# Moving weight subtractions off GpSimd and giving weight conversion fixed places in an attention and gated-MLP kernel

## The chip, the cores and the metric

The kernel runs on one core of a Trainium2 chip. The metric is the time of one execution in microseconds (us) on the device; the kernel before has a median of 754.77 us over three runs. A core has engines that work side by side, each through its own queue in order: TensorE (PE) multiplies matrices, VectorE (DVE) and GpSimd (POOL) do elementwise work, ScalarE (ACT) does activations and copies, SyncE (SP) and GpSimd issue the DMA transfers used here. Data lies in on-chip memory (SBUF) with 128 partitions; PE writes its sums to a second on-chip memory (PSUM).

## The reference

```python
# q, k, v: (4, 8, 576, 64)
scores = matmul(q, k.T) / sqrt(64)
rel = pos[:, None] - pos[None, :]
x = (log1p(abs(rel)) / log1p(max(pos, 1))[:, None])[..., None]
bias = relu(x @ w1 + b1) @ w2            # 32 hidden units, 8 heads
scores = scores + bias.transpose(2, 0, 1)[None]
attn = exp(scores - max(scores)); attn = attn / (sum(attn) + 1e-9)
x = (attn @ v).transpose(0, 2, 1, 3).reshape(2304, 512)
h = x @ w_in                             # (2304, 2048)
g = h * tanh(softplus(h))
out = g @ w_out                          # (2304, 512), float32
```

The weights w_in and w_out are double precision at the input, all else is float32.

## The kernel before

Every product is made of three: PE multiplies a rounded "high" part, which is fast, and a "low" part is the value minus its high part. So q, k, the weights, x and g are each split into hi and lo by a copy that rounds and a subtraction.

The program has three stages, each written out step by step, and each engine takes its work in the order of the code.

The bias stage, 0 to 62 us of the profiled run, makes a bias table per head from 36 groups of rows: DVE and ACT make ht (L488, L490), PE multiplies (bps, L517), ACT evacuates (L497, L498), and the table goes to DRAM and back. Between the groups lie the loads of the first two pairs of heads, the first three score steps (SOFT_AT), and the splits of q and k for pair 0 on DVE.

The attention stage, 62 to 326 us, goes over 16 pairs (two heads of one batch), five steps x = 0 to 4 each (n = 5i + x), which are the row blocks 0, 1, 4, 2, 3. A step does scores (L220, PE) into one of two PSUM buffers s, adds the bias and takes the row maxima on DVE (add_bias, L236, which frees s), exponentiates on ACT (L251), transposes the block of two steps earlier (PE L282 and L285, ACT copies L283, L289) and multiplies by v (L315, L319). The first product of step x = 2 is twelve matmuls long and serves as the mark of a pair below. At x = 4, load_hi and load_raw fetch q and k of the pair after the next. At x = 1 and x = 2, split_k and split_q on POOL subtract for the next pair: in the first pair both come at n = 3.

Beside this the weights are converted. A weight tile of 128x512 arrives as 64-bit words (load_weights, SP). Four operations make a float32: high (a multiplication, DVE L120 or ACT L118), low (a shift, DVE L123), a merge (DVE L125) and the sign (DVE L127). Then split_weights copies the high part (ACT L137) and subtracts for the low part on POOL (L138, tiles wli and wlo). 16 tiles are converted in the attention stage, one operation per step in a rotation of four steps that runs past the five of a pair; the other 16 are converted in the MLP. w64 and w32 have two buffers each.

The MLP, 326 to 752 us, goes over units of 12 matmuls for h (hidden, L594) and 12 for y (project, L632), where y lags three units behind h. Between the two, a gate: ACT exp (L599), DVE L600 and L601, ACT L609 and L610, DVE L611 and L612, ACT ghi (L613), and the subtraction for glo (L614), which runs on POOL for the first 23 units and on DVE after. Block 1 of x is split in the first eight units (split_x). The first segment's y accumulators are copied out (L639) after unit 7. convert() does a whole tile at the end of a unit: in three of four units from unit 8 on, in every second one before.

Of the kernel before, what the change touches and what calls it, by code (L numbers as in the profile page):

```python
# [19 lines left out]
P = 128  # L20
# [26 lines left out]
def kernel(ctx: ExitStack, tc, qk, v, wb, w2, w_in, w_out, psia, psi4, rinv, eye, out):  # L47
# [41 lines left out]
    todo, w64, w32 = list(order), [], []  # L89
# [17 lines left out]
    def conv_weights(on_act):  # L107

        job, w = w64.pop(0)
        c = convp.tile([P, 512], F32, name="w32")
        cu = c.bitcast(U32)
        high = convp.tile([P, 512], F32, name="high", bufs=1)
        low = convp.tile([P, 512], U32, name="low", bufs=1)
        hu = high.bitcast(U32)
        if on_act:
# [4 lines left out]
        def parts():  # L122
            dve.tensor_scalar(low, w[:, :, 0], 29, None, op0=ALU.logical_shift_right)  # L123
            yield False
            dve.scalar_tensor_tensor(cu, hu, 3, low, op0=ALU.logical_shift_left, op1=ALU.bitwise_or)  # L125
            yield False
            dve.scalar_tensor_tensor(cu, hu, 0x80000000, cu, op0=ALU.bitwise_and, op1=ALU.bitwise_or)  # L127
            w32.append((job, c))
            yield True
        return parts()  # L130
# [44 lines left out]
    def split_k(i):  # L175
        kl = qk_hi[i][64:128, QW:]
        (pool if i else dve).tensor_tensor(kl, qk_raw[i][64:128], kl.bitcast(F32), op=ALU.subtract)  # L177

    def split_q(i):

        lo = q_los[i % 2]
        (pool if i else dve).tensor_tensor(lo[0:64], qk_raw.pop(i)[0:64], qk_hi[i][0:64, :QW].bitcast(F32), op=ALU.subtract)  # L182
# [147 lines left out]
    conv = []  # L330
# [26 lines left out]

    def ahead(n):
# [18 lines left out]
    def split(n):  # L377
# [131 lines left out]
    for idx in range(NB + 2):  # L509
# [94 lines left out]
    def gate(blk, fs, eng=dve):  # L604
# [9 lines left out]
        eng.tensor_tensor(glo, e, ghi.bitcast(F32), op=ALU.subtract)  # L614
# [83 lines left out]
    done = []  # L698

    def convert():  # L700

        if done:
            split_weights(done.pop())
        if w64:
            for _ in conv_weights(True):
                pass
            load_weights()
            done.append(pool)

    gate(*units[0], pool)  # L710
    hidden(*units[1])
    convert()
    gate(*units[1], pool)
    hidden(*units[2])

    for k in range(2, len(units) + LAG2):
        if k < len(units):
            blk, fs = units[k]
            f = fs[0]
            if k < FH:  # L720
                split_x(1, XPARTS[:2] if k == 2 else XPARTS[2:4] if k == 3 else XPARTS[k:k + 1])
# [14 lines left out]
            if k > 2:  # L736
# [3 lines left out]
        if 2 <= k - 1 < len(units):  # L740
            gate(*units[k - 1], pool if k < 3 * FH else dve)
        if k > 2 and (k % 4 < 3 if k >= FH else k % 2):
# [58 lines left out]
```

## Time and profile before

| | us |
|---|---|
| median of three runs | 754.77 |
| runs | 753.52, 754.77, 756.04 |
| profiled execution, its own time | 754.99 |
| its span | 752.1 |
| busy: PE / DVE / ACT / POOL | 712.2 / 514.3 / 467.9 / 181.8 |

The span is the stretch from the first to the last instruction that the profiler recorded, and 2.9 us of the execution lie around it. Busy times say how much an engine did, not whether anybody waited for it; that is read from the chain that ended last, from the waits behind single rows, and from the timeline. The granted clock of TensorE is 1.00 at 2.4 GHz and 0.50 at 1.2 GHz; its mean in this execution is 0.986.

### The profile page before, as it was taken

What the parts mean: (1) busy time and instruction counts of PE and PEld (TensorE: products, weight loads), DVE (VectorE), ACT (ScalarE), POOL (GpSimd) and SP (SyncE); (2) the same over time, 40 slices, a digit from 0 to 9 for tenths busy, and PEclk for the clock granted to TensorE, in tenths of its full rate; (3) what the DMA queues carried; (4) which work ended last, traced back from release to release, by engine and by line L of the source; (5) the groups of instructions that cost most, each with busy time, mean ns of one, the idle gap of its engine ahead of it and who ended that gap; (6) DMA issues with size and microseconds to landing.
All of it is one profiled execution on the core that took longest, in us unless ns stands there. A gap on an engine that the chain in (4) does not pass through costs nothing.

```text
span 752.1 us, 11589 instructions
## 1 busy us (share of the span) xinstructions
PE 712.2 (95%) x4144; PEld 544.4 (72%) x4144; DVE 514.3 (68%) x987; ACT 467.9 (62%) x995; POOL 181.8 (24%) x113
## 2 busy tenths in 40 slices
PE   6769999999999999899989999999999999999997
PEld 2226777777777777658767776688998888888886
DVE  7995767768677764346877777777576666665554
ACT  6877877887888787665455455555454554444443
POOL 1110443565444453402343433300100000000000
PEclk9979999999999999999998999999999999999999
DMA  8987759648866977141113311132304000010001
GB/s 276 308 256 249 242 165 298 214 161 276 258 205 186 299 242 222 45 128 37 57 56 112 112 57 56 29 113 79 90 1 120 22 0 1 1 56 1 1 0 57
DMA packets 46681, 95.68 MB, mean 127 GB/s; under 512 B 13456, under 2 KB 22304, under 8 KB 44576
## 3 DMA queue, kind: packets, MB, share of 16 engines
q1 hardware_dynamic: 43744, 74.80, 32.9%
q0 software_dynamic: 2304, 19.92, 7.8%
q8 instruction: 32, 0.52, 0.3%
q10 hardware_dynamic: 576, 0.22, 0.1%
q14 instruction: 25, 0.20, 0.1%
HBM read 73.48 MB, written 21.45 MB: 126 GB/s over the span
## 4 chain that ended last, share of the span: by engine, by line
PE 66%; DVE 17%; ACT 8%; issue 4%; DMA 2%; POOL 2%; SPq 1%; DVEq 0%; ACTq 0%; POOLq 0%
PE y L632 18%; PE h L594 17%; PE s L220 11%; PE o L315 8%; PE tp L282 6%; DVE w L127 3%; PE bps L517 3%; DVE w L125 2%; DVE e L601 2%; DVE e L612 2%; DVE e L600 2%; PE o L319 2%; DVE e L611 2%; DMA xr<-r_d 2%; ACT high L118 1%
## 5 line engine op out<-in xcount | busy, mean ns | idle before, releaser
L251 ACT ACTIVATE pt<-pt,m 128x576 f32<-128x576 f32 x144 | 112.7, 784 | 53.0 <-DVE m L236 52.4
L236 DVE CUSTOM_DVE_ANT_0 pt<-s,bias 128x576 f32<-128x576 f32 x144 | 103.7, 752 | 55.3 <-PE s L220 53.5
L613 ACT CAST ghi<-e 128x512 fp32r<-128x512 f32 x72 | 44.7, 621 | 143.7 <-DVE e L612 139.7
L632 PE MATMUL y<-who,glo 128*128 128x512 f32 x288 | 114.4, 397 | 5.9 <-POOL glo L614 5.9
L632 PE MATMUL y<-who,ghi 128*128 128x512 f32 x288 | 114.1, 396 | 4.4 <-ACT xraw L639 2.2
L632 PE MATMUL y<-wlo,ghi 128*128 128x512 f32 x288 | 113.2, 393 | 0.0
L594 PE MATMUL h<-xhi,whi 128*128 128x512 f32 (+1 forms) x320 | 80.3, 372 | 1.0 <-ACT xhi L569 0.9
L594 PE MATMUL h<-xlo,whi 128*128 128x512 f32 (+1 forms) x320 | 79.0, 368 | 0.0
L594 PE MATMUL h<-xhi,wli 128*128 128x512 f32 (+1 forms) x320 | 78.8, 368 | 0.0
L220 PE MATMUL s<-qkhi 128*128 128x288 f32 x320 | 77.1, 322 | 0.7 <-issue 0.4
L315 PE MATMUL o<-main,vt 128*64 128x320 f32 (+1 forms) x512 | 75.8, 418 | 1.2 <-DVE x L322 1.2
L600 DVE TENSOR_SCALAR e<-e 128x512 f32<-128x512 f32 x72 | 36.5, 507 | 57.5 <-ACT e L599 57.5
L220 PEld LDWEIGHTS s<-qkhi 128*128 128x128 f32 x320 | 49.5, 189 | 34.1 <-issue 28.6
L220 PE MATMUL s<-qkhi,qlo 128*128 128x288 f32 x320 | 69.1, 297 | 3.6 <-POOL qlo L182 3.6
L177 POOL TENSOR_TENSOR qkhi<-rawqk,qkhi 64x1216 fp32r<-64x1216 f32 x15 | 42.7, 2844 | 118.5 <-DMA rawqk<-in_qk_dram 55.2
L632 PEld LDWEIGHTS y<-who,glo 128*128 128x128 f32 x288 | 54.6, 190 | 22.1 <-POOL glo L614 10.9
L599 ACT ACTIVATE e<-h 128x512 f32<-128x512 f32 x72 | 42.6, 591 | 43.5 <-PE h L594 43.5
L283 ACT COPY main<-tp 128x512 f32<-128x512 f32 x128 | 68.0, 581 | 0.7 <-PE tp L282 0.2
L632 PEld LDWEIGHTS y<-who,ghi 128*128 128x128 f32 x288 | 54.5, 189 | 19.0 <-ACT ghi L613 4.2
L282 PE MATMUL tp<-ident,pt 128*128 128x128 f32 x512 | 67.4, 275 | 0.7 <-ACT main L283 0.7
L594 PEld LDWEIGHTS h<-xhi,whi 128*128 128x128 f32 x320 | 57.8, 190 | 13.5 <-ACT xhi L569 2.4
L594 PEld LDWEIGHTS h<-xlo,whi 128*128 128x128 f32 x320 | 56.9, 189 | 10.4 <-DVE xlo L571 0.4
(75 smaller groups left out, 1210.6 us busy)
## 6 DMA issues: line engine op xcount, KB each, us to landing
qkhi<-in_qk_dram POOLq DMA_DIRECT2D x16, 1216.0 KB, 8.7
bias_d<-bt SPq DMA_DIRECT2D x36, 295.5 KB
rawqk<-in_qk_dram SPq DMA_DIRECT2D x32, 304.0 KB
w<-in_w_in_dram SPq DMA_DIRECT2D x16, 512.0 KB
w<-in_w_out_dram SPq DMA_DIRECT2D x16, 512.0 KB
vt<-in_v_dram SPq DMA_DIRECT2D x16, 320.0 KB
bias<-bias_d SPq DMA_DIRECT2D x16, 288.0 KB
out_dram<-w SPq DMA_DIRECT2D x17, 256.0 KB
```

The source lines that it names most:

```text
L177: (pool if i else dve).tensor_tensor(kl, qk_raw[i][64:128], kl.bitcast(F32), op=ALU.subtract)
L220: pe.matmul(s[:, j, :SH], stat[:, q0:q0 + P], hi[:, QW + kc + j * SH:QW + kc + (j + 1) * SH], start=(k == 0), stop=(k == len(todo) - 1))
L236: dve.tensor_tensor_reduce(out=halves(pt[:, sl]), in0=s[:, :, :SH], in1=halves(bt[:, sl]), scale=-0.125, scalar=BIG, op0=ALU.add, op1=ALU. ...
L251: act.activation(ps, ps, AF.Exp, bias=m[:, u:u + 1], scale=-1.0, accum_out=sums[i][:, k:k + 1])
L282: pe.transpose(tp[:, k * P:(k + 1) * P], pt[:, c0:c0 + P], ident)
L283: act.copy(main[:, h, :, off:off + P], tp.rearrange("p (k q) -> p k q", k=4))
L315: pe.matmul(o[h * 64:h * 64 + 64, :w], vt[:, h, k, :], main[:, h, k, :], start=(k == 0), stop=False, **kw)
L594: pe.matmul(h[:, u * n:(u + 1) * n], w["i", g4, d][:, r * P:(r + 1) * P], x[:, d, :n], start=(k == 0), stop=(k == 11))
L599: act.activation(e, h, AF.Exp)
L600: dve.tensor_scalar(e, e, E20, None, op0=ALU.min)
L613: act.copy(ghi, e)
L632: pe.matmul(ys[blk][t], g[:, c0:c0 + P], w, start=((blk, f) in first and k == 0), stop=((blk, f) in last and k == 2))
```

## The change

- The subtraction for wli and wlo (split_weights) moves from POOL to DVE, 32 instructions. That for glo of the first 23 MLP units does too. So do split_k and split_q of pair 1, and its split_q moves from n = 3 to n = 4. POOL keeps the splits of q and k of the pairs 2 to 15, the multiplications of x by the reciprocals, and two additions at the end.
- In the attention stage the operations of a tile have fixed steps: high and low at x = 4, followed by the load of the next tile; the merge at x = 0; the sign at x = 1; the copy of the high part and the subtraction at x = 2. The last tile goes through the steps n = 77 to 79.
- In the MLP, ACT's high stands at the start of a unit, low, merge and sign stand on DVE between L612 and the subtraction for glo, and the split of the tile comes at the start of the next unit. A tile is taken in units 0, 2, 4, 6, 7 and then in two of three units. The loop now starts with unit 0, and split_x of block 1 is spread over units 0 to 6.
- In the bias stage load_raw(1) moves from group 14 to 26, load_hi(1) from 18 to 28, the first load of weights from 26 to 30.

```diff
-    def conv_weights(on_act):
+    def scale_high(eng):
...
+    def shift_low():
+        job, w, high = half.pop(0)
+        low = convp.tile([P, 512], U32, name="low", bufs=1)
+        dve.tensor_scalar(low, w[:, :, 0], 29, None, op0=ALU.logical_shift_right)
+        half.append((job, high, low))
+        load_weights()
...
-    def split_weights(eng):
+    def split_weights():
         act.copy(w_hi[job], c)
-        eng.tensor_tensor(w_lo[job], c, w_hi[job].bitcast(F32), op=ALU.subtract)
+        dve.tensor_tensor(w_lo[job], c, w_hi[job].bitcast(F32), op=ALU.subtract)
...
     def split_k(i):
         kl = qk_hi[i][64:128, QW:]
-        (pool if i else dve).tensor_tensor(kl, qk_raw[i][64:128], kl.bitcast(F32), op=ALU.subtract)
+        (pool if i > 1 else dve).tensor_tensor(kl, qk_raw[i][64:128], kl.bitcast(F32), op=ALU.subtract)
...
-        if (x == 2 or n == 3) and i + 1 < NPAIR:
+        if (x == 2 or n == 4) and i + 1 < NPAIR:
             split_q(i + 1)
-        for _ in range((1, 1, 1, 1, 1)[x]):
-            if not conv and w64[0][0] in order[:HALF]:
-                conv.append(conv_weights(x == 2))
-            elif conv and next(conv[0]):
-                conv.clear()
-                load_weights()
-                split_weights(pool)
+        for do in CONV.get(n, {4: (scale_high, shift_low), 0: (merge,), 1: (sign,), 2: (split_weights,)}.get(x, ())):
+            do(*((dve,) if do is scale_high else ()))
...
-        if idx == 14:
+        if idx == 26:
             load_raw(1)
-        if idx == 18:
+        if idx == 28:
             load_hi(1)
-        if idx == 26:
+        if idx == 30:
             load_weights()
...
         act.copy(ghi, e)
-        eng.tensor_tensor(glo, e, ghi.bitcast(F32), op=ALU.subtract)
+        if half:
+            convert()
+        dve.tensor_tensor(glo, e, ghi.bitcast(F32), op=ALU.subtract)
...
-    for k in range(2, len(units) + LAG2):
+    for k in range(len(units) + LAG2):
+        on = k % 3 < 2 if k >= FH else k in (0, 2, 4, 6, 7)
+        if w32:
+            split_weights()
+        if on and w64:
+            scale_high(act)
...
-        if k > 2 and (k % 4 < 3 if k >= FH else k % 2):
+        if 0 <= k - 1 < len(units):
+            gate(*units[k - 1])
+        elif half:
             convert()
```

First place, DVE around step x = 2 of pair 11, before. L236 is add_bias, in two rows an instruction, L322 the copy of an attention output, L125 the merge; pt4 belongs to step 2, the last two s to step 3.

```order
L322 COPY x_3249<-o_3155 128x256
L236 ISA pt4_3262,m_3261<-s_3252,bias4_2410 128x576
L236 ISA m_3261 128x1
L125 SCALAR_TENSOR_TENSOR w32_3198<-high_3199,low_3200 128x512
L236 ISA pt_3305,m_3304<-s_3294,bias2_2453 128x576
L236 ISA m_3304 128x1
L236 ISA pt_3305,m_3304<-s_3299,bias2_2453 128x576
```

The same place after; lines have moved by eight or ten, so that add_bias is L244, the sign L136, and the subtraction for wlo L146.

```order
L136 SCALAR_TENSOR_TENSOR w32_3165<-high_3116,w32_3165 128x512
L330 COPY x_3214<-o_3122 128x256
L244 ISA pt4_3227,m_3226<-s_3217,bias4_2388 128x576
L244 ISA m_3226 128x1
L146 TENSOR_TENSOR wlo02_3252<-w32_3165,who02_3251 128x512
L244 ISA pt_3273,m_3272<-s_3262,bias2_2434 128x576
L244 ISA m_3272 128x1
L244 ISA pt_3273,m_3272<-s_3267,bias2_2434 128x576
```

Where before a step of the rotation stood, in this pair a merge, there now stands the subtraction, which needs ACT's copy who of the same step, between the add_bias of step 2 and the two of step 3.

Second place, DVE in a unit of the MLP that converts a tile, before. L600 to L612 belong to the gate, L123 to L127 to the conversion; the subtractions stand on POOL.

```order
L600 TENSOR_SCALAR e_4669<-e_4669 128x512
L601 SCALAR_TENSOR_TENSOR e_4669<-e_4669 128x512
L611 TENSOR_TENSOR e_4620<-h_4607,e_4620 128x512
L612 TENSOR_TENSOR e_4620<-e_4620,r_4685 128x512
L123 TENSOR_SCALAR low_4698<-w64_4565 128x512
L125 SCALAR_TENSOR_TENSOR w32_4696<-high_4697,low_4698 128x512
L127 SCALAR_TENSOR_TENSOR w32_4696<-high_4697,w32_4696 128x512
```

The same after. L603, L604, L619, L620 are the gate, L122, L129, L136 the conversion, L624 is glo and L146 a weight's low part.

```order
L603 TENSOR_SCALAR e_4722<-e_4722 128x512
L604 SCALAR_TENSOR_TENSOR e_4722<-e_4722 128x512
L619 TENSOR_TENSOR e_4682<-h_4669,e_4682 128x512
L620 TENSOR_TENSOR e_4682<-e_4682,r_4738 128x512
L122 TENSOR_SCALAR low_4746<-w64_4612 128x512
L129 SCALAR_TENSOR_TENSOR w32_4750<-high_4707,low_4746 128x512
L136 SCALAR_TENSOR_TENSOR w32_4750<-high_4707,w32_4750 128x512
L624 TENSOR_TENSOR glo_4740<-e_4682,ghi_4739 128x512
L146 TENSOR_TENSOR wli30_4335<-w32_4750,whi30_4334 128x512
```

DVE has two instructions more in such a unit, and the order of the seven others is kept.

Third place, SP in pair 13, where x of the first MLP block (xraw) and the reciprocals that it is multiplied by (xr) are loaded, before.

```order
L326 DMA x_d0_80<-x_3764 128x256
L327 DMA x_d0_80<-x_3764 128x64
L163 DMA rawqk_3799<-in_qk_dram 64x1216
L164 DMA rawqk_3799<-in_qk_dram 64x1216
L166 DMA vt_3802<-in_v_dram 128x640
L340 DMA xraw_3804<-x_d0_80 128x4x512
L354 DMA xr_3843<-r_d0_84 64x2x512 x2
```

The same after.

```order
L334 DMA x_d0_80<-x_3725 128x256
L335 DMA x_d0_80<-x_3725 128x64
L171 DMA rawqk_3760<-in_qk_dram 64x1216
L172 DMA rawqk_3760<-in_qk_dram 64x1216
L174 DMA vt_3763<-in_v_dram 128x640
L347 DMA xraw_3765<-x_d0_80 128x4x512
L104 DMA w64_3771<-in_w_out_dram 128x1024
L361 DMA xr_3810<-r_d0_84 64x2x512 x2
```

A load of a weight tile, 512 KB, now stands between xraw and xr.

## Rows read from the trace of the kernel before

**Rows 1.** The page, chain that ended last: shares of the span by engine.

```profile
PE 66%; DVE 17%; ACT 8%; issue 4%; DMA 2%; POOL 2%; SPq 1%; DVEq 0%; ACTq 0%; POOLq 0%
```

**Rows 2.** Windows: stretch, its length, busy us (instructions) per engine, clock, DMA share, GB/s.

```profile
62.00:326.00 264.00, 258.60 (x1903) 195.39 (x1902) 176.22 (x416) 209.52 (x533) 113.73 (x62) 0.99 0.69 212
326.00:521.00 195.00, 182.79 (x784) 141.59 (x782) 141.77 (x209) 101.55 (x180) 56.45 (x39) 0.98 0.23 72
```

**Rows 3.** Timeline (start, length, engine, line, operation, count, wait), PE in the MLP.

```profile
346.02 0.39 PE L632 MATMUL y<-who,ghi 128*128 128x512 f32 x1
348.74 1.07 PE L594 MATMUL h<-xhi,whi 128*128 128x512 f32 x4
...
390.57 1.07 PE L594 MATMUL h<-xhi,whi 128*128 128x512 f32 x4
...
520.52 0.64 PE L594 MATMUL h<-xhi,whi 128*128 128x256 f32 x4
```

**Rows 4.** Timeline, DVE, one group of the MLP.

```profile
421.79 1.67 DVE L127 SCALAR_TENSOR_TENSOR w<-high,w 128x512 uint32<-128x512 uint32 x1
...
425.22 0.69 DVE L612 TENSOR_TENSOR e<-e,r 128x512 f32<-128x512 f32 x1
425.83 0.42 DVE L123 TENSOR_SCALAR low<-w 128x512 uint32<-128x512 uint32 x1
...
428.62 1.67 DVE L127 SCALAR_TENSOR_TENSOR w<-high,w 128x512 uint32<-128x512 uint32 x1
```

**Rows 5.** Windows, the stretch after the first y accumulators are copied out.

```profile
396.00:402.80 6.80, 6.17 (x15) 4.38 (x14) 5.10 (x9) 3.19 (x7) 1.75 (x2) 0.50 0.55 208
```

**Rows 6.** Lines by shape, DVE, 35.3 to 41.2: busy us, mean ns.

```profile
L490 DVE TENSOR_SCALAR ht<-at,bb 128x304 f32<-128x304 f32 x3 | 5.9, 2010 | 0.0
```

**Rows 7.** The same, 41.2 to 50.7.

```profile
L490 DVE TENSOR_SCALAR ht<-at,bb 128x304 f32<-128x304 f32 x2 | 0.6, 359 | 0.0
```

**Rows 8.** Lines by shape, DVE, whole span.

```profile
L177 DVE TENSOR_TENSOR qkhi<-rawqk,qkhi 64x1216 fp32r<-64x1216 f32 x1 | 1.4, 1423 | 0.0
```

**Rows 9.** Timeline, POOL and DVE, conversion in the attention stage.

```profile
99.71 2.79 POOL L182 TENSOR_TENSOR qlo<-rawqk,qkhi 64x1216 fp32r<-64x1216 f32 x1
100.08 2.97 DVE L125 SCALAR_TENSOR_TENSOR w<-high,low 128x512 uint32<-128x512 uint32 x1
...
129.93 0.68 DVE L127 SCALAR_TENSOR_TENSOR w<-high,w 128x512 uint32<-128x512 uint32 x1
```

**Rows 10.** Timeline, ACT, DVE and PE, pair 13 from its step 2.

```profile
279.23 1.84 PE L315 MATMUL o<-main,vt 128*64 128x320 f32 x12
281.41 0.28 ACT L289 COPY tail<-tp 128x128 f32<-128x128 f32 x1
281.82 0.76 DVE L236 CUSTOM_DVE_ANT_0 pt<-s,bias 128x576 f32<-128x576 f32 x1 [2.16 <-PE s L220]
284.46 0.53 PE L220 MATMUL s<-qkhi 128*128 128x288 f32 x2
...
295.81 1.84 PE L315 MATMUL o<-main,vt 128*64 128x320 f32 x12
```

**Rows 11.** Timeline, ACT, the copy of a weight's high part.

```profile
131.91 0.64 ACT L137 CAST who<-w 128x512 fp32r<-128x512 f32 x1
```

**Rows 12.** Timeline, POOL: load of q and k issued, split of k.

```profile
169.71 0.57 POOL L172 DMA_DIRECT2D qkhi<-in_qk_dram  x1 [0.46 <-PE s L220]
178.84 3.16 POOL L177 TENSOR_TENSOR qkhi<-rawqk,qkhi 64x1216 fp32r<-64x1216 f32 x1 [3.38 <-DMA rawqk<-in_qk_dram]
...
219.77 0.57 POOL L172 DMA_DIRECT2D qkhi<-in_qk_dram  x1 [0.70 <-PE s L220]
229.66 2.80 POOL L177 TENSOR_TENSOR qkhi<-rawqk,qkhi 64x1216 fp32r<-64x1216 f32 x1 [1.93 <-DMA rawqk<-in_qk_dram]
...
286.09 0.57 POOL L172 DMA_DIRECT2D qkhi<-in_qk_dram  x1 [0.67 <-PE s L220]
```

**Rows 13.** Timeline, PE, pair 15's first use of qlo.

```profile
307.43 0.85 PE L220 MATMUL s<-qkhi,qlo 128*128 128x288 f32 x2 [2.92 <-POOL qlo L182]
```

More of the change, by code (lines that the diff above doesn't have):

```diff
@@ L88 @@
     w_hi, w_lo = {}, {}
-    todo, w64, w32 = list(order), [], []
+    todo, w64, half, w32 = list(order), [], [], []
     def alloc_weights(jobs, p):
@@ L105, in load_weights @@
             w64.append((job, w))
-    def conv_weights(on_act):
+    def scale_high(eng):
         job, w = w64.pop(0)
-        c = convp.tile([P, 512], F32, name="w32")
-        cu = c.bitcast(U32)
         high = convp.tile([P, 512], F32, name="high", bufs=1)
-        low = convp.tile([P, 512], U32, name="low", bufs=1)
-        hu = high.bitcast(U32)
-        if on_act:
+        if eng is act:
             act.mul(high, w.bitcast(F32)[:, :, 1], 2.0 ** -112)
@@ L120, in conv_weights, with merge, sign @@
             dve.tensor_scalar(high, w.bitcast(F32)[:, :, 1], 2.0 ** -112, None, op0=ALU.mult)
[L122 to L130, printed above, removed]
-    def split_weights(eng):
+        half.append((job, w, high))
+    def shift_low():
[4 more added lines that the diff above has]
+        load_weights()
+    def merge():
+        job, high, low = half.pop(0)
+        c = convp.tile([P, 512], F32, name="w32")
+        dve.scalar_tensor_tensor(c.bitcast(U32), high.bitcast(U32), 3, low,
+                                 op0=ALU.logical_shift_left, op1=ALU.bitwise_or)
+        half.append((job, high, c))
+    def sign():
+        job, high, c = half.pop(0)
+        cu = c.bitcast(U32)
+        dve.scalar_tensor_tensor(cu, high.bitcast(U32), 0x80000000, cu,
+                                 op0=ALU.bitwise_and, op1=ALU.bitwise_or)
+        w32.append((job, c))
+    def split_weights():
         job, c = w32.pop(0)
@@ L176, in split_k @@
         kl = qk_hi[i][64:128, QW:]
-        (pool if i else dve).tensor_tensor(kl, qk_raw[i][64:128], kl.bitcast(F32), op=ALU.subtract)
+        (pool if i > 1 else dve).tensor_tensor(kl, qk_raw[i][64:128], kl.bitcast(F32), op=ALU.subtract)
     def split_q(i):
         lo = q_los[i % 2]
-        (pool if i else dve).tensor_tensor(lo[0:64], qk_raw.pop(i)[0:64], qk_hi[i][0:64, :QW].bitcast(F32), op=ALU.subtract)
+        (pool if i > 1 else dve).tensor_tensor(lo[0:64], qk_raw.pop(i)[0:64], qk_hi[i][0:64, :QW].bitcast(F32), op=ALU.subtract)
         q_lo[i] = lo
@@ L329 @@
     LAG = 2
-    conv = []
     alloc_weights(order[:EARLY], wpool)
@@ L356, in load_r @@
                 off, m, s = off + k, m - k, s + k
+    CONV = {NS - 3: (split_weights, scale_high, shift_low), NS - 2: (merge, sign), NS - 1: (split_weights,)}
     def ahead(n):
@@ L602, in hidden, with convert, gate @@
         h_t[blk, fs] = (h, e)
-    def gate(blk, fs, eng=dve):
+    def convert():
+        shift_low()
+        merge()
+        sign()
+    def gate(blk, fs):
         r = mp.tile([P, TB], F32, name="r")
@@ L697 @@
     alloc_weights(order[HALF:], wq)
[L698 to L714, printed above, removed]
-    for k in range(2, len(units) + LAG2):
+    SHARE = {0: XPARTS[0:1], 1: XPARTS[1:2], 2: XPARTS[2:4], 3: XPARTS[4:5], 4: XPARTS[5:6], 5: XPARTS[6:7], 6: XPARTS[7:]}
+    for k in range(len(units) + LAG2):
[4 more added lines that the diff above has]
+            scale_high(act)
         if k < len(units):
@@ L720 @@
             if k < FH:
-                split_x(1, XPARTS[:2] if k == 2 else XPARTS[2:4] if k == 3 else XPARTS[k:k + 1])
+                split_x(1, SHARE.get(k, ()))
             elif blk == 1 and f == FH:
@@ L735 @@
                     split_x(blk + 1, XPARTS[f - 8:f - 8 + len(fs)])
-            if k > 2:
+            if k > 0:
                 hidden(blk, fs)
@@ L739 @@
             project(*units[k - LAG2])
-        if 2 <= k - 1 < len(units):
-            gate(*units[k - 1], pool if k < 3 * FH else dve)
-        if k > 2 and (k % 4 < 3 if k >= FH else k % 2):
+        if 0 <= k - 1 < len(units):
+            gate(*units[k - 1])
+        elif half:
             convert()
```

## The prediction

> **What bounds the kernel now.** I read the chain that ended last first: PE holds 66% of it, DVE 17%, POOL 2% [rows 1]. So PE sets the time over most of the span, and what can be won are the stretches in which it waits. The windows by stage say where they are. In the attention stage PE is busy 258.60 of 264.00 us; in the first part of the MLP 182.79 of 195.00, the lowest share, at a granted clock of 0.98 [rows 2]. There the reader is to compare PE's marks with its own pace. A block of twelve matmuls takes 348.74 - 346.02 = 2.72 us [rows 3]. From the first y at 346.02 to the h at 520.52, behind which nothing is converted, PE has 29 blocks of y and 28 of h to do: 57 x 2.72 = 155.0 us. It takes 174.5, so 19.5 are lost. Who takes them stands on DVE: with a conversion in the unit, the sign operation comes at 421.79 and again at 428.62, 6.83 us apart [rows 4], where PE wants 2 x 2.72 = 5.44. The sign itself takes 1.67 there and 0.68 alone [rows 4, 9].
>
> The same price has its cause in plain sight in the attention stage: the merge begins at 100.08 and takes 2.97, while the subtraction of q on POOL runs from 99.71 to 102.50 [rows 9]. It ends at 103.05, 0.55 after POOL. So a DVE operation with both inputs in SBUF stands still until POOL's subtraction is over. In the bias stage the same thing: three ht of 128x304 take 5.9 us while POOL splits pair 1, and 0.359 each afterwards [rows 6, 7].
>
> **The change part by part.** The sum is made against the profiled execution, 754.99 us with its span of 752.1 and 2.9 around it; that is 0.22 above the median.
>
> MLP. DVE gets two subtractions more in a unit, but POOL no longer stands in its way. With 0.69 for an operation with two inputs, 0.42 for one with one [rows 4] and 0.68 for merge and sign [rows 9], the gate with glo costs 0.42 + 4 x 0.69 = 3.18, a conversion 0.42 + 2 x 0.68 = 1.78, a weight's low part 0.69. Three units hold two conversions: 3 x 3.18 + 2 x (1.78 + 0.69) = 14.5 us, and PE wants 16.3. PE becomes the bound. Not at once: a conversion and parts of split_x now stand ahead of the first gate, and I give the eight first blocks of y no gain, so that PE is again at 390.57 [rows 3]. From there 42 blocks are left to the mark: 114.2, to 504.8. Behind that point the first y accumulators are copied out, where PE stops and then runs 6.8 us at a clock of 0.50 [rows 5]; I leave 3.0 for this. The mark comes at 507.8 instead of 520.5: **-12.7**. Bounds: -16.5 if only the 3.0 of the copy-out stay of the 19.5, -9 if the longer chain of a unit (glo after the conversion) still keeps PE waiting by a quarter of a microsecond in some sixteen units.
>
> Bias stage. 5.9 - 3 x 0.359 = 4.8 us of standing go away with the two splits of pair 1. ht feeds PE, but the tables' stores and loads may set the end, and the loads of pair 1 come later. No row tells these apart: between -4.8 and +1; I take half of the former, **-2.4**.
>
> Step 5. split_q(1) takes 1.42 on DVE, by the only subtraction of this form there, split_k(0) [rows 8]. It stands behind the add_bias of step 4; PE's scores of step 5 wait for the buffer that the next add_bias frees. **+1.4**, between 0 (hidden) and 2.2 (with the add_bias of 0.76 [rows 10] behind it).
>
> The subtraction for wlo at x = 2, the term that decides. I count from the mark of a pair, 279.23 for pair 13, the next being at 295.81, 16.58 later [rows 10]. ACT ends its copy of tail at 281.69, +2.46; the copy who takes 0.64 [rows 11]; so DVE can subtract from +3.10. Queued behind it on DVE are the two add_bias of step 3; the first takes 0.76 [rows 10] and frees the buffer that PE wants at 284.46, +5.23. DVE has to be done with wlo by about +4.4. Alone, at 0.69, it would be done at +3.8, and the cost is nothing. But where is POOL then? It starts to split k of the next pair 9.13 to 9.89 us after the load of q and k is issued (169.71 to 178.84, 219.77 to 229.66), and the issue stands at +6.86 (286.09) [rows 12]; from the next mark that is -0.6 to +0.2. With 2.80 for k and 2.79 for q [rows 9, 12], q is under way from some +2.3 to +3.0 until +5.1 to +5.8. The request at +3.10 falls into it. If the subtraction waits as the merge did, it ends 0.55 after POOL, at +5.6 to +6.4; the add_bias ends at +6.4 to +7.1; PE waits 1.1 to 1.9, 1.5 in the middle. This pair by pair: POOL splits in pairs 2 to 13 beside a conversion, twelve times. In the three in which bias tables are loaded too, the split should start later and wlo get in first, which I estimate without a row. Nine times 1.5 is **+13.5**. Bounds: 0, with wlo at 0.69 as L612 is [rows 4], which is the same operation on the same shape, but with POOL idle; 12 x 1.9 = 23. I take the upper side because the nearest row in the circumstances, two SBUF inputs on DVE during a subtraction of POOL, is the merge of 2.97.
>
> The Trainium skill, page "SBUF — State Buffer", section "SBUF: two separate sides", says that an operation of VectorE with two SBUF inputs and one of GpSimd that reads SBUF share a pair of ports, which is held like a lock for a whole instruction, so that the other one stands fully blocked. By that rule the subtraction on DVE is held as the merge was, and the change, which leaves the splits on POOL, doesn't end the collisions at x = 2; without it the sum would be lower by the 13.5. The merge at 100.08 agrees; no row shows a plain subtraction held.
>
> Pair 15. SP now issues a weight tile of 512 KB ahead of xr. At the stage's 212 GB/s [rows 2] that is 2.5 us. The multiplications by xr stand on POOL ahead of the split of q of pair 15, for which PE already waits 2.92 [rows 13]. **+2.0**, between 0 (other engines' transfers leave room) and 2.5.
>
> Into the MLP. At n = 79 the copy who (0.64) and a subtraction (0.69) stand ahead of work for the first h: **+0.6**, between 0 and 1.3.
>
> The other moved operations of the attention stage (high and low at x = 4, merge at x = 0, sign at x = 1) I cost at nothing. They stand behind the add_bias of their step, and POOL is idle there, its split of q being over at the latest at +5.8, ahead of the scores of x = 4. If that cover goes, each is worth at most what the merge lost, 2.3.
>
> Sum: -12.7 - 2.4 + 1.4 + 13.5 + 2.0 + 0.6 = +2.4, 757.4; less 0.2 to the median, **757**.
>
> **The rivals.** *Wlo is not held* (faster). A plain subtraction runs beside POOL, or POOL's split comes so late that wlo gets in ahead of q. For it: L612 never took more than its 0.69 in rows; against it: the merge. The time is 757 - 13.5 = 743.5. It decides from a split that starts after +0.24, since then q starts after +3.1.
>
> *Half of the pairs are caught.* The spread of the split's start, 0.8 us, ends close to the point of decision, and the fixed weight load at x = 4 shares the transfers with q and k. Six pairs less or a stop of half the length: 757 - 6.8 = 750.
>
> *The stops lower the clock* (slower). The stop at the copy-out was followed by 6.8 us at 0.50, which cost 3.4 [rows 5]. If the stops of 1.1 to 1.9 do the same to the nine pairs, at half that price, it is 9 x 1.7 = 15 more: 772. Against it: no row shows a half clock after stops that short. It decides as soon as the clock is 0.50 after one of these stops.
>
> **How the numbers follow.** My forecast 0.46, with a range of its own from 752 to 762; wlo not held 0.28; half 0.14; clock 0.12. The range of 743 to 768 holds the first three and the lower part of the last. A measurement tells 0.3%, 2.3 us, from no change. Faster than that: nearly all of 0.28, 0.11 of 0.14, and 0.06 of the forecast, in all 0.45. Slower: 0.12, and 0.22 of the forecast, 0.34. The remaining 0.21 is the same.
>
> **What would show it.** Right: in the timeline of a middle pair, a subtraction L146 on DVE of 2 to 3 us at x = 2 while POOL splits q, behind it PE waiting for DVE at the scores of x = 4, and marks 18 us apart instead of 16.58. Wrong: L146 at 0.7 us and marks 16.6 apart, and a time near 744. For the MLP: the sign at 0.7 us in every unit, units of 5.44, and the h that follows the last conversions some 12 to 13 us nearer to the first y. If units with a conversion still take over 6 us, this term is wrong, and the time is near 765. For the bias stage: ht at 0.4 us throughout, and the first mark 1 us earlier, the 2.4 less the 1.4.

## The result and the profile after

The changed kernel is slower: 760.27 us median of 16 runs (755.78 to 766.94) against 754.48 (751.37 to 757.27, 16 runs), a ratio of 1.0084 with a 95% interval of 1.0055 to 1.0113. The prediction was 757 with a range of 743 to 768, slower by 0.3%. The profiled execution took 759.74, its span is 758.0. The runs of the changed kernel spread over 11 us, those of the kernel before over 6; the six longest of the former (763.22 to 766.94) have a mean granted clock of 0.982 to 0.984, the five shortest (755.78 to 757.69) one of 0.986 to 0.991. Cut at the same marks as before, one profiled execution against the other:

| stretch | before | after | difference | forecast |
|---|---|---|---|---|
| start to the mark of pair 1 | 78.57 | 80.51 | +1.9 | -1.0 |
| mark of pair 1 to that of pair 14 | 217.24 | 232.36 | +15.1 | +13.5 |
| pair 14 to pair 15 | 21.28 | 23.18 | +1.9 | +2.0 |
| pair 15 to the first y | 28.93 | 32.00 | +3.1 | +0.6 |
| first y to the h at the end of conversion | 174.50 | 158.81 | -15.7 | -12.7 |
| from there to the end | 231.58 | 231.14 | -0.4 | 0 |
| span | 752.1 | 758.0 | +5.9 | +2.4 |

So a gain of 15.7 us in the MLP stands against a loss of 15.1 in the attention stage and 6.9 around it. The windows of after show the same stretches; the columns are those of [rows 2].

```profile
80.51:312.87 232.36, 220.16 (x1601) 162.24 (x1600) 154.80 (x366) 171.91 (x444) 83.04 (x40) 1.00 0.70 205
312.87:336.05 23.18, 19.69 (x124) 14.60 (x123) 13.48 (x29) 13.41 (x34) 10.15 (x6) 0.85 0.42 129
336.05:368.05 32.00, 27.73 (x160) 18.73 (x159) 17.95 (x39) 18.19 (x41) 0.00 (x0) 1.00 0.42 118
368.05:526.86 158.81, 156.62 (x685) 128.09 (x685) 134.60 (x227) 92.73 (x159) 0.00 (x0) 1.00 0.22 70
526.86:758.00 231.14, 227.36 (x1093) 191.74 (x1091) 141.72 (x229) 108.93 (x179) 2.60 (x2) 1.00 0.12 35
```

PE's clock is 1.00 from the first pair's mark to the fourteenth's, and 0.85 in the stretch behind it. PE is busy 156.6 of 158.8 us in the MLP stretch, and only 220.2 of 232.4 in the attention stage. The chain that ended last has gained DMA and ACT against [rows 1], and lost PE and DVE:

```profile
PE 60%; DVE 12%; ACT 10%; DMA 6%; issue 5%; SPq 1%; POOL 1%; ACTq 0%; DVEq 0%; POOLq 0%
```

The waits of PE by releaser, of after (engine, line, releaser: us, times, longest):

```profile
PE s L228 <- DVE m L244: 12.9, 13, 1.5
PE s L228 <- POOL qlo L190: 3.5, 1, 3.5
PE tp L290 <- ACT main L291: 3.4, 2, 3.2
PE s L228 <- DVE qlo L190: 1.6, 1, 1.6
```

The first row is the new one: scores that wait for the row maxima of add_bias, thirteen times.

One pair of after from its mark, in the timeline, answers to [rows 10] and [rows 11]:

```profile
276.36 2.77 POOL L185 TENSOR_TENSOR qkhi<-rawqk,qkhi 64x1216 fp32r<-64x1216 f32 x1 [8.63 <-DMA rawqk<-in_qk_dram]
276.84 1.84 PE L323 MATMUL o<-main,vt 128*64 128x320 f32 x12
...
279.18 0.64 ACT L145 CAST who<-w 128x512 fp32r<-128x512 f32 x1
279.20 2.78 POOL L190 TENSOR_TENSOR qlo<-rawqk,qkhi 64x1216 fp32r<-64x1216 f32 x1
...
279.85 2.68 DVE L146 TENSOR_TENSOR wlo<-w,who 128x512 fp32r<-128x512 f32 x1 [2.58 <-ACT who L145]
...
282.45 0.74 DVE L244 CUSTOM_DVE_ANT_0 pt<-s,bias 128x576 f32<-128x576 f32 x1
...
283.26 0.53 PE L228 MATMUL s<-qkhi 128*128 128x288 f32 x2 [1.12 <-DVE m L244]
...
294.96 1.84 PE L323 MATMUL o<-main,vt 128*64 128x320 f32 x12
```

The reader is to follow it from the mark at 276.84. ACT's copy who ends at 279.82, +2.98. DVE starts its subtraction at 279.85 and takes 2.68 for it, since POOL has begun its split of q at 279.20 and keeps at it until 281.98. The subtraction ends at 282.53, 0.55 after POOL, just as the merge in [rows 9]. The add_bias behind it starts at 282.45, and PE gets its buffer at 283.26, +6.42 instead of +5.23, after a wait of 1.12 put down to DVE. The next mark comes 18.12 us after this one instead of 16.58. Eleven of the thirteen pairs have such a wait, of 0.9 to 1.5 us, 12.2 in all; with small gaps among the matmuls behind each wait, 0.35 in this pair, the eleven are 16.8 longer than 16.58 each. The difference to before is 15.1, since before lost 1.7 in its own pairs 1, 2, 4 and 6, which took 16.69 to 17.55; pair 2 is the one with the held merge of [rows 9]. In the two others of after, pairs 1 and 4, the request came just as POOL went from k to q, and DVE got in between. Then it is POOL that is held, 3.35 and 3.17 instead of 2.78; the first of the two:

```profile
84.05 0.69 DVE L146 TENSOR_TENSOR wli<-w,whi 128x512 fp32r<-128x512 f32 x1 [2.58 <-ACT whi L145]
84.05 3.35 POOL L190 TENSOR_TENSOR qlo<-rawqk,qkhi 64x1216 fp32r<-64x1216 f32 x1
```

In the MLP the first y and the h behind the conversions, as in [rows 3]:

```profile
368.05 0.50 PE L642 MATMUL y<-who,ghi 128*128 128x512 f32 x1 [1.07 <-ACT ghi L621]
...
526.86 0.64 PE L597 MATMUL h<-xhi,whi 128*128 128x256 f32 x4
```

And DVE in units there, as in [rows 4]:

```profile
419.55 0.69 DVE L136 SCALAR_TENSOR_TENSOR w<-high,w 128x512 uint32<-128x512 uint32 x1
...
429.53 0.69 DVE L136 SCALAR_TENSOR_TENSOR w<-high,w 128x512 uint32<-128x512 uint32 x1
430.14 0.68 DVE L624 TENSOR_TENSOR glo<-e,ghi 128x512 fp32r<-128x512 f32 x1
430.91 0.69 DVE L146 TENSOR_TENSOR wli<-w,whi 128x512 fp32r<-128x512 f32 x1
```

The sign takes 0.69 instead of 1.67, glo and the weight's low part 0.68 and 0.69, and the two signs, two units apart, lie 9.98 us from each other, within the 10.88 that PE needs for the four blocks of two units.

In the bias stage, seven ht of 128x304 take 0.359 each; this answers to [rows 6] and [rows 7]:

```profile
L493 DVE TENSOR_SCALAR ht<-at,bb 128x304 f32<-128x304 f32 x7 | 2.2, 359 | 0.0
```

DVE is no longer held there. But further on it waits for a bias table, which it did not do before, and PE waits for what follows from that (3.20, behind which the granted clock was 0.50 from 65.0 to 68.4 us) and for split_q(1):

```profile
62.04 0.76 DVE L244 CUSTOM_DVE_ANT_0 pt<-s,bias 128x576 f32<-128x576 f32 x1 [2.84 <-DMA bias<-bias_d]
...
64.23 1.37 PE L290 MATMUL tp<-ident,pt 128*128 128x128 f32 x8 [3.20 <-ACT main L291]
...
73.76 0.50 PE L228 MATMUL s<-qkhi,qlo 128*128 128x288 f32 x2 [1.56 <-DVE qlo L190]
```

### The profile page after: what moved, and what is told of

It is laid out like the page before. It is cut to its first block, busy times and chain, and to the rows that moved or that the text cites. A ratio compares the mean times of both kernels' runs of the same rounds, so it can differ in the third digit from the quotient of the medians.

```text
span 758.0 us, 11563 instructions
## 1 busy us (share of the span) xinstructions
PE 709.2 (94%) x4144; PEld 543.6 (72%) x4144; DVE 523.7 (69%) x1047; ACT 465.6 (61%) x992; POOL 99.9 (13%) x56
## 4 chain that ended last, share of the span: by engine, by line
PE 60%; DVE 12%; ACT 10%; DMA 6%; issue 5%; SPq 1%; POOL 1%; ACTq 0%; DVEq 0%; POOLq 0%
PE y L642 23%; PE h L597 22%; PE s L228 6%; PE o L323 4%; DVE pt L244 4%; ACT main L291 3%; ACT pt L259 3%; PE tp L290 2%; DMA x_d<-x 2%; DMA bias_d<-bt 2%; DMA xr<-r_d 2%; DVE w L136 1%; PE tp L303 1%; DMA w<-in_w_out_dram 1%; DVE e L620 1%
## 5 line engine op out<-in xcount | busy, mean ns | idle before, releaser
L244 DVE CUSTOM_DVE_ANT_0 pt<-s,bias 128x576 f32<-128x576 f32 x144 | 103.4, 749 | 37.6 <-PE s L228 34.6
L642 PE MATMUL y<-who,ghi 128*128 128x512 f32 x288 | 112.5, 391 | 2.2 <-ACT ghi L621 1.4
L642 PE MATMUL y<-who,glo 128*128 128x512 f32 x288 | 112.4, 390 | 1.0 <-DVE glo L624 1.0
L597 PE MATMUL h<-xhi,whi 128*128 128x512 f32 (+1 forms) x320 | 79.7, 369 | 1.8 <-ACT xhi L572 1.7
L624 DVE TENSOR_TENSOR glo<-e,ghi 128x512 fp32r<-128x512 f32 x72 | 49.7, 691 | 42.0 <-ACT ghi L621 42.0
L603 DVE TENSOR_SCALAR e<-e 128x512 f32<-128x512 f32 x72 | 30.6, 425 | 54.5 <-ACT e L602 54.5
L597 PEld LDWEIGHTS h<-xhi,wli 128*128 128x128 f32 x320 | 56.9, 189 | 10.0
```

Source lines behind the costliest of these rows:

```text
L244: dve.tensor_tensor_reduce(out=halves(pt[:, sl]), in0=s[:, :, :SH], in1=halves(bt[:, sl]), scale=-0.125, scalar=BIG, op0=ALU.add, op1=ALU. ...
L597: pe.matmul(h[:, u * n:(u + 1) * n], w["i", g4, d][:, r * P:(r + 1) * P], x[:, d, :n], start=(k == 0), stop=(k == 11))
L603: dve.tensor_scalar(e, e, E20, None, op0=ALU.min)
L624: dve.tensor_tensor(glo, e, ghi.bitcast(F32), op=ALU.subtract)
L642: pe.matmul(ys[blk][t], g[:, c0:c0 + P], w, start=((blk, f) in first and k == 0), stop=((blk, f) in last and k == 2))
```

## The experiments

Ratios are of each kernel to the kernel before, with their 95% intervals.

**e1: the copy and the subtraction at x = 3.** Theory: POOL holds the subtraction on DVE, and it costs since add_bias of step 3 is queued behind it. Rivals: DVE has too much to do; the weight tile loaded at x = 4 delays q and k.

```diff
-{4: (scale_high, shift_low), 0: (merge,), 1: (sign,), 2: (split_weights,)}
+{4: (scale_high, shift_low), 0: (merge,), 1: (sign,), 3: (split_weights,) if w32 else ()}
```

> The changed kernel, with one edit: in the attention stage the copy of a weight's high part and the subtraction for its low part stand at x = 3 instead of x = 2; the same instructions on the same engines. Theory (the subtraction on DVE is held by POOL's split of q, and what it costs is the place: the add_bias of step 3 stands behind it): at x = 3 the copy comes some 3.5 us later, when POOL's split is over, the subtraction takes 0.7 us, PE's eleven waits of 0.9 to 1.5 us at the scores of x = 4 are gone, the marks of the pairs stand 16.6 us apart instead of 17.9 to 18.5, and the time falls by 13 to 15 us to 745 to 748. Rival (DVE simply has more to do in the attention stage than it has room for, or the fixed load of a weight tile at x = 4 delays q and k): the marks stay about 18 us apart and the time stays within 4 us of 760.

Measured: 753.52 (752.26 to 755.47), ratio 0.9995 (0.9978 to 1.0013), and marks 17.34 apart, in every pair alike. That is half of what the theory said, and neither side's number. The timeline of a pair of e1 says why:

```profile
276.53 0.62 ACT L145 CAST who<-w 128x512 fp32r<-128x512 f32 x1
...
277.18 0.69 DVE L146 TENSOR_TENSOR wlo<-w,who 128x512 fp32r<-128x512 f32 x1 [2.72 <-ACT who L145]
...
277.79 0.48 DVE L330 COPY x<-o 128x320 f32<-128x320 f32 x1
...
278.33 1.08 PE L323 MATMUL o<-main,vt 128*64 128x256 f32 x8 [0.69 <-DVE x L330]
```

The subtraction takes 0.69, POOL is over. But it begins only when ACT has made its copy, late in the step, and DVE, which takes its work in order, waits for that. Behind it stands the copy of the attention output (L330), and for this one PE waits 0.69, in thirteen pairs. So neither rival: an operation that isn't ready costs what stands behind it, whether POOL holds it or ACT is late.

**e2: the subtraction on POOL in the attention stage.**

```diff
-            do(*((dve,) if do is scale_high else ()))
+            do(*((dve,) if do is scale_high else (pool,) if do is split_weights else ()))
```

> The changed kernel, with one edit: the subtraction for a weight's low part in the attention stage is on POOL again, behind the split of q of the same step; the MLP keeps it on DVE. Theory (held behind POOL): marks 16.6 us apart and a time of 745 to 748, as with the subtraction moved to x = 3, although DVE has 0.69 us a pair less to do here. Rival (DVE has too much to do): this one is clearly faster than the subtraction moved to x = 3, which then stays near 760. Rival (the fixed weight load delays q and k): both stay near 760.

Measured: 741.99 (739.44 to 743.40), ratio 0.9838 (0.9808 to 0.9867), below the 745 to 748 of the theory, with marks 16.58 apart in every pair. Of the 18 us against the change, 16.8 lie between the marks of pairs 1 and 14. The fixed weight load is still at x = 4 here, so that this rival falls. That DVE has too much to do was not excluded by e1 and e2 together.

**e5: copy at x = 3, subtraction at x = 4, on DVE.**

```diff
-2: (split_weights,)
+3: (copy_high,) if w32 else ()          # act.copy alone
-4: (scale_high, shift_low)
+4: ((sub_low,) if copied else ()) + (scale_high, shift_low)
```

> The changed kernel, with the subtraction for a weight's low part still on DVE in the attention stage, but split from its copy: ACT copies at x = 3, DVE subtracts at x = 4, ahead of high and low. With both at x = 3 the subtraction was not held (0.69 us), but DVE waited for ACT's copy with the copy of the attention output behind it, and PE waited 0.69 a pair for that. Theory (neither the lock nor DVE's load costs by itself, but what is queued behind an operation that is not yet free to run): here the copy is long done and POOL idle, so the subtraction takes 0.69 without a wait, the marks stand 16.6 us apart, and the time is 741 to 744, as with the subtraction on POOL. Rival (DVE's 0.69 more in a pair costs by itself): marks at 17.2 or more, 750 or more.

Measured: 743.36 (742.34 to 747.23), ratio 0.9853 (0.9809 to 0.9896), marks 16.58 apart. The subtraction runs right behind its step's add_bias, without a wait:

```profile
270.33 0.62 ACT L147 CAST who<-w 128x512 fp32r<-128x512 f32 x1
...
271.65 0.69 DVE L152 TENSOR_TENSOR wlo<-w,who 128x512 fp32r<-128x512 f32 x1
```

DVE does exactly what it does in the changed kernel, and the attention stage is as fast as with POOL. DVE's load is out as a cause.

**e6: copy at x = 1, subtraction at x = 2.** This one keeps the subtraction held.

```diff
-1: (sign,), 2: (split_weights,)
+1: (sign, copy_high), 2: (sub_low,)
```

> The changed kernel, with the copy of a weight's high part at x = 1 and the subtraction at x = 2 as before, so that DVE can ask for it right behind the add_bias of step 2, some 0.7 us after the mark of a pair instead of 3.1. Theory (what costs is that the request falls into POOL's split of q and is held to its end): the subtraction is held still, by the split of k, and takes 1.5 to 2.9 us, but gets in between the splits of k and q and ends by +3.6 after the mark, before DVE is wanted at +4.4; the marks stand 16.6 us apart and the time is 741 to 746. Rival (being held costs, wherever it ends): the subtraction still takes over 2 us in most pairs, the marks stay at 17.5 or more, and the time stays over 753.

Measured: 743.40 (740.98 to 746.00), ratio 0.9840 (0.9793 to 0.9887), marks 16.58 apart with one of 17.06.

```profile
263.83 0.62 ACT L147 CAST who<-w 128x512 fp32r<-128x512 f32 x1 [0.18 <-DVE w L136]
263.93 2.78 POOL L195 TENSOR_TENSOR qkhi<-rawqk,qkhi 64x1216 fp32r<-64x1216 f32 x1 [8.47 <-DMA rawqk<-in_qk_dram]
...
264.74 2.52 DVE L152 TENSOR_TENSOR wlo<-w,who 128x512 fp32r<-128x512 f32 x1
...
266.79 3.11 POOL L200 TENSOR_TENSOR qlo<-rawqk,qkhi 64x1216 fp32r<-64x1216 f32 x1
...
267.18 0.74 DVE L254 CUSTOM_DVE_ANT_0 pt<-s,bias 128x576 f32<-128x576 f32 x1
```

The subtraction is asked for 0.37 after the mark of 264.37 and takes 2.52, about as long as in the changed kernel (2.45 to 3.08). It is held by the split of k, though, gets in between k and q, and ends at +2.89, ahead of the add_bias that PE wants. Being held costs nothing by itself; the point in time at which it ends costs. In twelve of the fourteen pairs it is held by the split of k, and one of the two others has the 17.06.

**e7 and e8: POOL or the new places in the MLP.** e7 is the changed kernel with the MLP's subtractions on POOL, e8 the kernel before with them on DVE.

```diff
-            gate(*units[k - 1])
+            gate(*units[k - 1], pool if k < 24 else dve)
-            split_weights()
+            split_weights(pool)
```

> The changed kernel, with the subtractions of the MLP on POOL again (glo of the first 23 units and the weights' low parts), everything else and the order as changed. Theory (the gain in the MLP comes from POOL no longer holding DVE up): the stretch from the first y to the h behind the last conversions, 158.8 us with the change and 174.5 without it, is back at 170 us or more. Rival (the gain comes from the new places, with the conversion inside the wait for ghi and a tile in two of three units instead of three of four): it stays under 164 us.

Measured: 776.24 (772.48 to 780.04), ratio 1.0280 (1.0222 to 1.0337). First y and the h behind the conversions in e7:

```profile
363.00 0.45 PE L642 MATMUL y<-who,ghi 128*128 128x512 f32 x1
...
539.60 0.64 PE L597 MATMUL h<-xhi,whi 128*128 128x256 f32 x4
```

176.6 us: without POOL's release the new places gain nothing, they lose 2.1.

```diff
-            gate(*units[k - 1], pool if k < 3 * FH else dve)
+            gate(*units[k - 1])
-            split_weights(done.pop())
+            done.pop()
+            split_weights(dve)
```

> The kernel before, with one part of the change alone: the subtractions of the MLP on DVE (glo of the first 23 units and the weights' low parts), all in the places of before. Theory (off POOL is what counts): the stretch from the first y to the h behind the last conversions falls from 174.5 us to 163 or less, the time by 10 us or more. Rival (the new places are what counts): it stays over 168 us, since three of four units then hold 5.6 us of work on DVE against PE's 5.44.

Measured: 742.01 (740.45 to 743.49), ratio 0.9826 (0.9775 to 0.9877). The same in e8:

```profile
346.00 0.39 PE L632 MATMUL y<-who,ghi 128*128 128x512 f32 x1
...
509.96 0.64 PE L594 MATMUL h<-xhi,whi 128*128 128x256 f32 x4
```

163.96: 10.5 of the 15.7 us come from taking POOL out of DVE's way, and the places add 5.2 once it is out. The expectation's 163 was missed by one; on the whole both matter, in this order. The sizes are those of single executions: that of before has 6.8 us at a clock of 0.50 in this stretch, which cost 3.4 [rows 5], and those of after, e7 and e8 have none.

**e9: the MLP part of the change alone.** The attention and bias stages are those of before; the loop, gate() and convert() of the MLP are the changed ones (the diff of the change from def convert() on).

> The kernel before, with the whole MLP part of the change (subtractions on DVE, conversion inside the wait for ghi, two of three units, loop from unit 0) and nothing else of it; bias and attention stages as before. Theory (the MLP part gains some 15 us by itself, all that the change lost lies in the two other stages and the passage from one to the other): marks of the pairs as before (16.6 apart, the first at 78 to 79), the stretch from the first y to the h behind the last conversions 159 us, time 738 to 742. Rival (part of the 3 us lost between the last mark and the first y belongs to the MLP part, which puts a conversion ahead of the first gate): the first y comes over 1.5 us later after the last mark than the 28.9 of before.

Measured: 741.41 (736.59 to 742.77), ratio 0.9818 (0.9782 to 0.9855). The MLP stretch takes 158.83, as with the whole change. From the mark of pair 15 (314.03) to the first y (344.15) it is 30.1, 1.2 more than before: of the 3.1 lost there, 1.2 belong to the MLP part. The other 1.9 come with the rest of the change.

**e3 and e10: the loads of the bias stage back.** e3 does it in the changed kernel, e10 in e5.

```diff
-        if idx == 26:
+        if idx == 14:
             load_raw(1)
-        if idx == 28:
+        if idx == 18:
             load_hi(1)
-        if idx == 30:
+        if idx == 26:
             load_weights()
```

> The changed kernel, with one edit: in the bias stage the loads of pair 1 and of the first weights are back at groups 14, 18 and 26 (from 26, 28 and 30). Theory A (the gain of 4 to 5 us from taking the splits of pair 1 off POOL was there at 45 us and was lost again, since the moved loads fill the transfers from 44 to 62 us and the last bias tables land late): the first mark of a pair comes at 77 to 78 us instead of 80.5, and the time falls by 2 to 4 us. Theory B (the transfers of the whole stage are the bound, wherever the loads stand): the first mark stays at 80 to 81, the time within 1 us.

Measured: 757.59 (750.16 to 763.51), ratio 1.0035 (1.0007 to 1.0063), first mark at 78.08. The time fits theory A, but its interval meets that of the change, and the number of pairs that are caught at x = 2 differs between executions: e3's profile has three marks 16.58 apart. It also has one of 21.25, in pair 12, where the clock fell behind a wait of the same kind; the wait, and the window behind it with the columns of [rows 2]:

```profile
281.71 0.53 PE L228 MATMUL s<-qkhi 128*128 128x288 f32 x2 [1.69 <-DVE m L244]
```

```profile
282.55:285.95 3.40, 3.40 (x16) 2.64 (x18) 2.31 (x7) 3.39 (x11) 0.71 (x1) 0.50 0.46 131
```

Hence e10.

> The changed kernel with ACT's copy at x = 3 and the subtraction at x = 4 (743.4 us), and in the bias stage the loads of pair 1 and of the first weights back at groups 14, 18 and 26. Without the waits at x = 2, whose number changes from run to run, a difference in the bias stage can be seen. Theory A (the moved loads make the bias tables late): first mark at 77 to 78.5 instead of 78.4 to 81.8 in the kernels with the loads at 26 to 30, time 739.5 to 742. Theory B (the stage is bound by its transfers wherever the loads stand): within 1 us of 743.4.

Measured: 739.68 (738.27 to 744.16), ratio 0.9809 (0.9778 to 0.9841), first mark at 76.77. By the times alone the interval meets that of e5. By the first mark it is clear enough: 76.1 to 78.1 in the four kernels with the loads at 14 to 26 and the splits on DVE, 78.4 to 81.8 in the seven with the loads at 26 to 30, 78.6 to 79.0 in the three with the bias stage of before. Theory A stands: the splits on DVE gain about 2 us, the moved loads cost about 3. Part of the 3 is the clock. With the moved loads and no half clock ahead of the first mark (e2, e7) it comes at 78.4, 1.4 to 2.3 later than in e10, e11 and e12; the five others with the moved loads have 0.50 for some us there and come at 79.7 to 81.8.

**e4 and e11: the weight tile behind xr.** e4 does it in the changed kernel, e11 in e10.

```diff
+        if n == NS - 10:
+            load_weights()       # not in shift_low() at n = NS - 11
```

> The changed kernel, with one edit: the load of a weight tile at n = 69, which stands ahead of the first load of the reciprocals xr on SP, is issued behind it at n = 70. Theory: xr lands some 2 us earlier, POOL's multiplications and behind them its split of q of pair 15 come earlier, PE's wait of 3.5 us there shrinks to under 2 us, and the time falls by 1.5 to 3 us. Rival (xr's rows are fetched slowly for another reason, as its many small pieces, and the weight load does not matter): the wait stays at 3 us or more and the time within 1 us.

Measured: 757.66 (752.01 to 764.12), ratio 1.0036 (1.0003 to 1.0069). PE's wait is 2.16, a little over the 2 of the theory, and the stretch from pair 14 to 15 takes 20.6. The time is 2.6 lower, with an interval that meets that of the change. That looks like the theory, but the landing does not. SP's issues and the first multiplication on POOL, which waits for xr, in e4:

```profile
305.49 1.37 SPq L362 DMA_DIRECT2D xr<-r_d  x2
306.90 0.86 SPq L104 DMA_DIRECT2D w<-in_w_out_dram  x1
```

```profile
317.69 2.54 POOL L385 TENSOR_TENSOR xraw<-xraw,xr 128x512 f32<-128x512 f32 x2 [3.30 <-DMA xr<-r_d]
```

and with the tile ahead, in the changed kernel:

```profile
305.96 0.65 SPq L104 DMA_DIRECT2D w<-in_w_out_dram  x1
306.66 1.34 SPq L361 DMA_DIRECT2D xr<-r_d  x2
```

```profile
319.42 2.70 POOL L384 TENSOR_TENSOR xraw<-xraw,xr 128x512 f32<-128x512 f32 x2 [4.48 <-DMA xr<-r_d]
```

xr takes 12.2 us from its issue to its use here, and 12.8 there: 0.6 less, not 2. Counted from the mark of pair 14, it is used at +5.37 here and at +6.55 there, the issue being 0.6 earlier as well.

> As the kernel with copy at x = 3, subtraction at x = 4 and the loads of the bias stage back, and the weight tile of n = 69 loaded behind xr. Theory: PE's wait for qlo of pair 15, 3.5 to 4.0 us with the tile ahead, is under 2.2, the stretch between the marks of pairs 14 and 15 some 1.5 to 2.5 us shorter than with the tile ahead, and the time lower by the same. Rival (the wait is made up later, since the second half of xr and the multiplications set when the first xhi is ready): the stretch is shorter, but the first y comes no earlier, and the time is the same.

Measured: 739.04 (736.38 to 741.96), ratio 0.9796 (0.9764 to 0.9828), against e10's 739.68. PE's wait is 4.28, longer than e10's 3.88, and the stretch 22.5 against 23.3. The theory falls: the tile's place changes little. In the four kernels with the attention stage of before (before, e8, e9, e12), which issue no tile there, xr takes 12.5 to 13.6, and in e1, with the tile ahead, only 9.1. What sets it stays open; no run changed the small pieces.

**e12: the parts that gain.** The kernel e9 with the splits of pair 1 on DVE, its loads where they were.

```diff
-        (pool if i else dve).tensor_tensor(kl, ...)
+        (pool if i > 1 else dve).tensor_tensor(kl, ...)
-        (pool if i else dve).tensor_tensor(lo[0:64], ...)
+        (pool if i > 1 else dve).tensor_tensor(lo[0:64], ...)
-        if (x == 2 or n == 3) and i + 1 < NPAIR:
+        if (x == 2 or n == 4) and i + 1 < NPAIR:
```

> The kernel before with the MLP part of the change, and of the rest only the splits of q and k of pair 1 on DVE (q at n = 4); its loads stay at groups 14, 18 and 26, and the attention stage keeps its rotation with the subtractions on POOL. Theory (the stages add up: first mark at 76.8, as in the kernel with the loads back; 216 us to the mark of pair 14 and 49 from there to the first y, as in the kernel with the MLP part alone; 159 and 231 after that): a span of some 732 and a time of 734 to 737, faster than every kernel so far. Rival (the first mark does not come earlier here, since the split of q costs its 1.4 at step 5 and POOL's hold on ht cost nothing, or what comes earlier is lost again in the loads of pair 2): the time stays at 739 to 742.

Measured: 737.63 (735.67 to 739.39), ratio 0.9789 (0.9752 to 0.9827), the fastest median of all, though its interval meets those of all the kernels near 740 (e2, e5, e6, e8 to e11). Its marks of pairs 1 and 15, first y and end of conversion:

```profile
76.10 1.83 PE L357 MATMUL o<-main,vt 128*64 128x320 f32 x12
...
312.50 1.83 PE L357 MATMUL o<-main,vt 128*64 128x320 f32 x12
...
342.89 0.50 PE L681 MATMUL y<-who,ghi 128*128 128x512 f32 x1 [1.07 <-ACT ghi L660]
...
501.73 0.64 PE L636 MATMUL h<-xhi,whi 128*128 128x256 f32 x4
```

The first mark came as forecast, at 76.1 for 76.8, the span is 733.5 for 732. The median is 0.6 above the range that was expected.

## Why the prediction was right, and where it was not

The forecast was slower by a little, with the loss at x = 2 against the gain in the MLP. Both are there, and the place is the one named. That the median lies only 3 above the 757 is in part luck: the terms around the two came out some 5 us dearer in all, and the MLP 3 cheaper. By its terms:

- *The subtraction at x = 2, +13.5; measured +15.1.* Right in each step: the request at +3.10 (+3.01 in the pair shown), held until 0.55 after POOL's split of q, 1.1 to 1.9 a pair (0.9 to 1.5 of wait, 1.3 to 1.9 with the gaps behind it). e6 shows that it is the end of the hold that costs, as the step said. What failed is the count: "Nine times 1.5" left out the three pairs with bias tables, since a later split should let DVE in. The pairs that load them, 3, 7 and 11, were caught, with waits of 0.91, 1.52 and 0.91; a later split came, if at all, in the pair behind, 4, 8 or 12. Pair 4 did get in free. In pair 8 the split of k started at +2.5, and the request at +3.0 fell into this one instead; PE waited 1.25. Pair 12 was caught like the rest, and pair 1, which the forecast did not count, got in. The point of decision held: the splits of k in the two free pairs start after the +0.24 of the forecast, at +0.66 and +0.33, and all others but that of pair 8 start before it. The right count was eleven of thirteen. At 1.5 each that is 16.8, and the +15.1 is less because before lost 1.7 in four pairs, which the forecast left out.
- *MLP, -12.7; measured -15.7.* The mechanism is right (e7, e8), the size too small: the 3.0 left for the copy-out of the first y were not used up, the wait there fell from 2.18 and 0.63 to 0.84, and the half clock of [rows 5] did not come.
- *Bias stage and step 5, -1.0 together; measured +1.9.* Step 5 is right, PE waits 1.56 for DVE's qlo against the 1.4 forecast. The gain from the splits is right too, about 2 (e10, and e12 against e9). The step that failed is the bound "+1" for the loads that come later: they cost about 3 over the kernels, half clock included, since they fall among the last bias tables, and DVE waited 2.84 for one of these.
- *Pair 15, +2.0; measured +1.9.* The size is luck and the reason wrong. xr did not land later by 2.5 us, but was used 6.55 us after the mark of pair 14 where it had been 6.36. And the stretch differs as much between executions of the same attention stage: 21.28, 20.91, 18.75 and 19.60 in before, e8, e9 and e12, of which the last two have no half clock there. Between the two profiles compared, PE's wait grew from 2.92 [rows 13] to 3.49, and the half clock behind it lasted longer:

```profile
325.05 0.85 PE L228 MATMUL s<-qkhi,qlo 128*128 128x288 f32 x2 [3.49 <-POOL qlo L190]
```

Windows of the half clock behind this wait, of after and then of before:

```profile
325.05:331.20 6.15, 6.15 (x25) 4.67 (x26) 4.16 (x7) 2.97 (x7) 2.51 (x2) 0.50 0.35 109
```

```profile
307.40:310.70 3.30, 3.27 (x14) 3.26 (x15) 2.16 (x6) 1.45 (x3) 1.38 (x2) 0.50 0.21 51
```

6.2 us at 0.50 instead of 3.3 is 1.4 us more of PE's time, and with 0.57 of wait that is about the 1.9.
- *Into the MLP, +0.6; measured +3.1.* Undersized. 1.2 of it is the conversion ahead of the first gate (e9), which the forecast put at nothing by counting the first y's from 390.57 on; of the other 1.9, the waits show 1.2: PE waits 1.73 for ACT's xhi instead of 0.94, and 0.44 for ACT's main, which it did not before. No run took those apart.

Of the rivals, "wlo is not held" falls with the 2.68. "The stops lower the clock" does not hold for the profiled execution, with its 1.00 from pair 1 to pair 14, but it is not gone: in e3 a stop of 1.69 was followed by 3.4 us at 0.50, and one of 1.66 in the same execution by none. "Half of the pairs are caught" has a grain: two of thirteen got in here, three in e3. Both the number caught and the lower clock of the longest runs fit the spread of the changed kernel's runs; no run separated the two.

The sentence on the Trainium skill, page "SBUF — State Buffer", section "SBUF: two separate sides": this case's traces agree that a plain subtraction on DVE with two SBUF inputs is fully held (2.68 for 0.69), and that whichever comes first keeps the other one out (POOL 3.35 for 2.78 when DVE was first).

## What to carry to other kernels

Price an operation that another engine can hold up by what is queued behind it and when that is wanted, not by how long it is held: the same instruction of some 2.5 us cost 1.5 us in each pair caught at one place, and nothing when it was asked for 2.6 us earlier. Where such an operation needs another engine's result, put it a step behind that result, so that its own engine never waits for it. And test a change by its parts, since here the part that lost was as large as the part that gained, and a few lines in one table separated 760 from 743.

## What the runs showed of the hardware that was not expected

- A held operation shows no wait in the profile, it is only longer. The 2.68 us count as busy time of DVE, whose busy share says 69% in a kernel in which it stands still eleven times.
- DVE gets in between two operations of POOL that follow each other without a gap: in e6 it ran between the splits of k and q in eleven pairs, and POOL's split of q was then recorded with 3.11 to 3.13 instead of 2.78.
- Eleven waits of 0.9 to 1.5 us, 18 us apart, left PE's clock at 1.00; a single one of 3.49 was followed by 6.2 us at 0.50, one of 2.92 by 3.3. The length of the wait alone does not decide: one of 1.69 (e3) was followed by 3.4 us at 0.50, one of 2.75 (e12) by none.
